# Linear attention into a gated MLP on one core: first weight block in two halves, far chunks projected in pairs, inputs stored in load order

## The chip, the cores and the metric

The kernel runs on one core of one Trainium2 chip. The metric is device time in microseconds (us) from launch to end; lower is better. The five engines are named as in the profile: PE (TensorE), ACT (ScalarE), DVE (VectorE), POOL (GpSimd) and SP (SyncE, which here only issues DMAs).

## What is computed

```
# q, k, v: (4, 4, 1088, 32); S1, S2: (8, 32); w_in: (128, 2048); w_out: (2048, 128)
def phi(x):                                  # 8 x 8 = 64 features
    a = einsum('rd,bhsd->bhsr', S1, x); b = einsum('rd,bhsd->bhsr', S2, x)
    return einsum('bhsi,bhsj->bhsij', a, b).reshape(..., 64)
q_p, k_p = phi(q), phi(k)
kv = einsum('bhsf,bhsd->bhfd', k_p, v);  z = sum(k_p, axis=2)
num = einsum('bhsf,bhfd->bhsd', q_p, kv)
den = einsum('bhsf,bhf->bhs', q_p, z)[..., None] + 1e-06
x = (num / den) with heads side by side      # (4352, 128)
h = x @ w_in;  g = h * clip(h + 3, 0, 6) / 6;  out = g @ w_out
```

## The kernel before

The 4352 tokens are cut into 9 chunks (`CHUNKS`, lines 38 and 39): eight of 512 tokens and a last one of 256. The keys and values of the four batches come in two groups per batch (`KGROUPS`, k0 to k7 and v0 to v7). All inputs lie in DRAM in pieces, one DMA each, and are loaded by SP (line 323).

The attention part has three kinds of step. `keys(b)` (from line 397) makes the key features of a batch (`mm_k`, `cp_k`, `outer_k`), sums them with the values over nine tiles (`kvt_b_i`, lines 405 and 408) and folds the sum into two small matrices (`twice`, `fold`, `keep`; for batch 0 also `spread`, `zmm`, `halves`, lines 427 to 436). `queries(c)` serves chunk 0 alone (`mm_q0`, `outer_q0`, `tr`, `nd`, `norm`, `xt`, lines 475 to 518). `far_queries(c)` serves chunks 1 to 8 (line 520): `proj_c` (line 533) projects one chunk on PE with small 32x32 matmuls into two banks of PSUM, DVE transposes them (`cp`, line 536), POOL and DVE form quotient and features (`prod`, `invert`, `divide`, `outer`, `turn`), eight small DMAs move them (`move_c`, line 574), and `xmm_c` (line 579) multiplies with the folded sum, again small matmuls of one chunk into two banks. `split` then writes x as a high and a low part (`xhi`, `xlo`).

The MLP part has 72 steps, one for each chunk c and pair fp of the eight pairs of 128 columns of w_in. In a step PE makes h from three products (`h_` and `l_`: lines 608, 609, 612), ACT and DVE make the gate (`relu`, line 619; `gate`, line 622), ACT rounds it (`ghi`, line 625), POOL or DVE takes the rest (`glo`, line 628), and PE adds six products with w_out to the chunk's sum (`o_` and `p_`, line 645). These matmuls use the whole array; below they are called the dense ones, and the small ones of attention the tiled ones.

The weights arrive as 64-bit floats in blocks of 512 columns (wi0 to wi3, wo0 to wo3) and are turned by hand into two 32-bit parts, seven instructions a block: `scale` and `rest` on ACT (lines 337, 340), `sign` and `shift` on DVE (343, 347), `word` on POOL (351), `high` on ACT (354), `low` on POOL (357). A step with pair fp waits for its block.

Three 16-element loads on ACT's queue (`peek`, line 258) touch three inputs at the start. Nothing is scheduled by the compiler: `ORDER` (lines 97 to 157) is a list of step names, and each engine and SP's queue take their instructions in that order. A suffix (`:V`, `:h`) picks an engine or a bank. `Plan.run` (line 189) gives each step its buffers from `BUFS`, first free first.

Of the kernel before, what the change touches and what calls it, by code (L numbers as in the profile page):

```python
# [97 lines left out]
warm ld_q0 warm warm mm_q0 ld_k0 cp_q0 ld_k1 mm_k0:h cp_k0 ld_v0 ld_wi1 ld_v1 outer_q0_0:V mm_k1 cp_k1 tr_0_0:o trcp_0_0 rest_wi1 scale_wi1 s_rep  # L98
s_copy outer_k1_0 outer_k0_2:V outer_k0_0:V outer_q0_2:V outer_k1_2:V outer_k1_4 kvt_0_0 kvt_0_1 kvt_0_2 s_tr kvt_0_3 kvt_0_4 kvt_0_5 kvt_0_6 kvt_0_7
kvt_0_8 s_back twice_0 fold_0 sign_wi1:h shift_wi1 spread zmm tr_0_2 word_wi1 ld_wi0 rest_wi0 scale_wi0 sign_wi0:o shift_wi0 word_wi0 halves nd_0_0:o  # L100
trcp_0_2 keep_0 high_wi1 ld_q1 ld_wo1 ld_k2 ld_k3 high_wi0 nd_0_2:h ld_wi2 low_wi1 norm_0_0 proj_1 xt_0_0:o ld_v2 low_wi0 ld_v3 ld_k4 ld_wi3 norm_0_2
xt_0_2 xhi_0_1 xhi_0_0 cp_1_0 mm_k2 ld_k5 cp_1_1 ld_wo0 sign_wo1:o scale_wo1 cp_k2 mm_k3 cp_k3 rest_wo1 prod_1 xlo_0_1 xlo_0_0 h_0_3_0 l_0_3_0 h_0_3_1
l_0_3_1 outer_k2_0 shift_wo1 h_0_0_1_0 l_0_0_1_0 h_0_0_1_1 l_0_0_1_1 h_0_0_0_0 invert_1 outer_k3_4:V outer_k2_2:V kvt_1_0:o kvt_1_1 l_0_0_0_0
h_0_0_0_1 sign_wi2 relu_0_3 word_wo1 scale_wi2 divide_1 outer_1_1 outer_1_0 gate_0_3 l_0_0_0_1 h_0_2_1 l_0_2_1 h_0_2_0 shift_wi2 outer_k3_0:V
outer_k3_2:V kvt_1_2 kvt_1_3 kvt_1_4 kvt_1_5 kvt_1_6 rest_wi2 relu_0_0 high_wo1 ghi_0_3 word_wi2 kvt_1_7 kvt_1_8 twice_1 high_wi2 mm_k4 l_0_2_0
low_wo1 fold_1 o_0_3 turn_1_0 turn_1_1 gate_0_0 h_0_1_1_0 low_wi2 l_0_1_1_0 h_0_1_1_1 h_0_1_0_0 l_0_1_1_1 l_0_1_0_0 move_1 h_0_1_0_1 l_0_1_0_1
relu_0_2 keep_1 scale_wi3 cp_k4 rest_wi3 sign_wi3:o ld_q3 gate_0_2 h_0_4_0 l_0_4_0 h_0_4_1 l_0_4_1 glo_0_3 mm_k5 ghi_0_2 p_0_3 o_0_2 outer_k4_0:V
shift_wi3 outer_k4_2:V word_wi3 relu_0_1 scale_wo0 cp_k5 relu_0_4 high_wi3 ld_v4 ld_q2 ld_v5 ghi_0_0 sign_wo0:o gate_0_1 h_0_5_1 h_0_5_0 l_0_5_1
l_0_5_0 relu_0_5 outer_k5_4:V outer_k5_0:V outer_k5_2:V xmm_1 xhi_1_0 glo_0_2 low_wi3 p_0_2 xhi_1_1 rest_wo0 gate_0_4 h_0_6_1 l_0_6_1 h_0_6_0 l_0_6_0
relu_0_6 ghi_0_4 shift_wo0 xlo_1_0 xlo_1_1 gate_0_5 proj_3 kvt_2_0 kvt_2_1 kvt_2_2 kvt_2_3 glo_0_0 word_wo0 high_wo0 low_wo0 h_1_2_0 h_1_2_1 l_1_2_1  # L110
l_1_2_0 relu_1_2 cp_3_0 ghi_0_1 gate_0_6 h_1_1_0 l_1_1_0 h_1_1_1 l_1_1_1 glo_0_4:V relu_1_1 cp_3_1 gate_1_2 kvt_2_4 kvt_2_5 kvt_2_6 kvt_2_7 proj_2
kvt_2_8 o_0_1 ld_q8 ld_v6 ld_k7 ld_wo2 ld_wo3 ld_q5 glo_0_1:V gate_1_1 ghi_1_2 h_1_3_1 h_1_3_0 l_1_3_0 l_1_3_1 ghi_1_1 relu_1_3 twice_2 scale_wo2
h_1_0_1 l_1_0_1 p_0_1 h_1_0_0 o_0_0 p_0_0 prod_3 invert_3 cp_2_0 fold_2 glo_1_2:V divide_3 rest_wo2 outer_3_1 glo_1_1 outer_3_0 cp_2_1 l_1_0_0 keep_2
prod_2 o_1_2 proj_5 gate_1_3 sign_wo2:h shift_wo2 word_wo2 ghi_1_3 relu_1_0 turn_3_1 cp_5_0 h_0_7_1 l_0_7_1 h_0_7_0 o_1_1 l_0_7_0 gate_1_0 h_1_5_0
invert_2 h_1_5_1 l_1_5_0 glo_1_3:V ghi_0_6 relu_0_7 p_1_2 l_1_5_1 cp_5_1 o_1_3 p_1_1 high_wo2 relu_1_5 out_0_3 divide_2 ghi_0_5 low_wo2 gate_0_7
h_1_4_0 turn_3_0 h_1_4_1 l_1_4_1 gate_1_5 p_0_4 l_1_4_0 h_1_7_0 h_1_7_1 l_1_7_0 ghi_1_0 glo_0_5:V scale_wo3 relu_1_4 rest_wo3 sign_wo3 shift_wo3
gate_1_4 ld_q4 ld_v7 ld_k6 move_3 ld_q6 o_0_4 p_0_5 ghi_0_7 proj_4 o_0_5 outer_2_1 glo_1_0 word_wo3 ghi_1_5 high_wo3 outer_2_0 low_wo3 cp_4_1 cp_4_0
# [619 lines left out]
```

## Time and profile before

| | |
|---|---|
| median of 3 runs | 230.46 us (230.12 to 230.94) |
| the profiled execution's own time | 230.75 us |
| its span, first to last instruction | 229.0 us |
| PE busy | 221.2 us, 97% of the span |
| DVE, ACT, POOL busy | 73%, 72%, 66% of the span |
| read from HBM | 11.30 MB |

The span is what the trace covers; 1.75 us of the profiled execution lie outside it. PE's busy time counts matmuls with their modelled ends, so two that overlap in the pipeline count once, and a high share does not say that each matmul runs at its best pace.

### The profile page before, as it was taken

The page shows a single profiled execution, that of the slowest core. Times are in us where ns is not written, and L with a number is a line of the kernel's source. Part 1 is how long each engine was busy: PE and PEld are TensorE (multiplying, and loading weights), DVE is VectorE, ACT ScalarE, POOL GpSimd, SP SyncE. Part 2 cuts the span into 40 slices and gives each one's busy share as a digit, 9 for nine tenths or more (in the row PEclk, how much of TensorE's full clock was granted, in tenths as well). Part 3 has the DMA queues.
Part 4 walks back from the last instruction along what each step waited for, and adds up shares of the span by engine and source line. Part 5 has one row for each costly group of instructions (what it writes and reads, how often), then busy time and mean ns, then how long its engine had stood idle before and what let it go on. Part 6 is the DMA issues. An engine that isn't in the chain of part 4 may idle for free.

```text
span 229.0 us, 4745 instructions
## 1 busy us (share of the span) xinstructions
PE 221.2 (97%) x1880; PEld 174.4 (76%) x1880; DVE 166.7 (73%) x215; ACT 166.0 (72%) x228; POOL 151.0 (66%) x108
## 2 busy tenths in 40 slices
PE   4899999999999999999999999999999999999994
PEld 2767867768687788777778788787888788888984
DVE  1789999999779768548869968885483577575552
ACT  3579998869778776877578666687585866778662
POOL 3289998496994599996077754037749615776480
PEclk9999999999999999999999999999999999999999
DMA  6995249701412001401200031212002000001001
GB/s 204 401 407 173 61 134 345 265 3 34 105 33 61 0 3 34 151 3 29 66 0 1 3 91 48 92 26 69 0 23 69 3 0 0 37 11 46 0 4 69
DMA packets 9382, 17.77 MB, mean 78 GB/s; under 512 B 1808, under 2 KB 2448, under 8 KB 9360
## 3 DMA queue, kind: packets, MB, share of 16 engines
q1 hardware_dynamic: 9264, 17.46, 23.0%
q8 instruction: 15, 0.25, 0.4%
q14 instruction: 7, 0.06, 0.1%
q10 hardware_dynamic: 96, 0.00, 0.0%
HBM read 11.30 MB, written 2.23 MB: 59 GB/s over the span
## 4 chain that ended last, share of the span: by engine, by line
PE 91%; DVE 2%; DMA 2%; ACT 2%; issue 1%; SPq 1%; ACTq 0%
PE o L645 42%; PE h L608 14%; PE h L612 13%; PE h L609 13%; PE a L579 2%; DMA kT<-kT_dram 2%; PE o L405 2%; PE a L533 2%; PE a L375 2%; ACT r L340 1%; DVE g L622 0%; PE o L489 0%; DVE kph L385 0%; DVE x L507 0%; SPq L323 0%
## 5 line engine op out<-in xcount | busy, mean ns | idle before, releaser
L628 POOL TENSOR_TENSOR gl<-g,gh 128x1024 fp32r<-128x1024 f32 (+1 forms) x41 | 95.7, 2349 | 49.6 <-ACT gh L625 31.9
L622 DVE SCALAR_TENSOR_TENSOR g<-g,h 128x1024 f32<-128x1024 f32 (+1 forms) x72 | 82.8, 1155 | 44.4 <-ACT g L619 44.1
L619 ACT ACTIVATE g<-h 128x1024 f32<-128x1024 f32 (+1 forms) x72 | 70.3, 981 | 34.1 <-PE h L612 21.7
L625 ACT CAST gh<-g 128x1024 fp32r<-128x1024 f32 (+1 forms) x72 | 70.9, 1003 | 13.0 <-PE o L645 6.6
L608 PE MATMUL h<-xh,wi_hi 128*128 128x512 f32 (+1 forms) x148 | 56.0, 380 | 0.5 <-DVE g L622 0.5
L645 PE MATMUL o<-gh,wo_hi 128*128 128x512 f32 (+1 forms) x144 | 54.9, 384 | 0.0
L609 PE MATMUL h<-xh,wi_lo 128*128 128x512 f32 (+1 forms) x148 | 54.9, 373 | 0.0
L645 PE MATMUL o<-gh,wo_lo 128*128 128x512 f32 (+1 forms) x144 | 54.1, 378 | 0.0
L612 PE MATMUL h<-xh,wi_hi 128*128 128x512 f32 (+1 forms) x148 | 51.1, 375 | 0.0
L645 PE MATMUL o<-gl,wo_hi 128*128 128x512 f32 (+1 forms) x144 | 41.3, 380 | 0.0
L628 DVE TENSOR_TENSOR gl<-g,gh 128x1024 fp32r<-128x1024 f32 (+1 forms) x31 | 38.2, 1244 | 2.4 <-ACT gh L625 2.3
L608 PEld LDWEIGHTS h<-xh,wi_hi 128*128 128x128 f32 x148 | 27.8, 188 | 8.2 <-DVE g L622 1.1
L645 PEld LDWEIGHTS o<-gh,wo_hi 128*128 128x128 f32 x144 | 27.1, 188 | 6.5 <-issue 0.8
L612 PEld LDWEIGHTS h<-xh,wi_hi 128*128 128x128 f32 x148 | 27.5, 188 | 5.3
L609 PEld LDWEIGHTS h<-xh,wi_lo 128*128 128x128 f32 x148 | 27.8, 188 | 4.8
L645 PEld LDWEIGHTS o<-gh,wo_lo 128*128 128x128 f32 x144 | 27.1, 188 | 4.8
L645 PEld LDWEIGHTS o<-gl,wo_hi 128*128 128x128 f32 x144 | 25.8, 188 | 5.4 <-issue 0.8
L562 POOL TENSOR_TENSOR qph<-ab 128x512 f32<-128x512 f32 (+1 forms) x16 | 19.9, 1257 | 0.3
L351 POOL TENSOR_TENSOR w<-w,r 128x512 int32<-128x512 int32 x8 | 10.3, 1290 | 1.9 <-DVE w L347 1.9
L569 DVE STREAM_TRANSPOSE raw<-qph 128x512 f32<-128x512 f32 (+1 forms) x16 | 10.5, 665 | 0.3 <-POOL qph L562 0.3
L543 POOL TENSOR_TENSOR prods<-ab 128x128 f32<-128x128 f32 (+1 forms) x8 | 4.5, 557 | 7.0 <-DVE den L547 5.0
L385 POOL TENSOR_TENSOR kph<-ab 128x512 f32<-128x512 f32 (+1 forms) x6 | 5.5, 928 | 4.2 <-ACT ab L378 4.2
(95 smaller groups left out, 162.5 us busy)
## 6 DMA issues: line engine op xcount, KB each, us to landing
phT<-raw SPq DMA_DIRECT2D x56, 64.0 KB, 2.0
qT<-qT_dram SPq DMA_DIRECT2D x8, 256.0 KB, 3.1
raw<-w_in_dram SPq DMA_DIRECT2D x4, 512.0 KB, 7.7
raw<-w_out_dram SPq DMA_DIRECT2D x4, 512.0 KB, 7.0
outT_dram<-os SPq DMA_DIRECT2D x8, 256.0 KB, 2.2
v<-v_dram SPq DMA_DIRECT2D x4, 330.0 KB, 5.1
kT<-kT_dram SPq DMA_DIRECT2D x4, 320.0 KB, 5.1
v<-v_dram SPq DMA_DIRECT2D x4, 264.0 KB, 5.0
```

Source lines behind the costliest of these rows:

```text
L351: nc.gpsimd.tensor_tensor(w, w, at(rb), op=ALU.add)
L385: engines[e].tensor_tensor(out, a_, b_, op=ALU.mult)
L562: engines[e].tensor_tensor(out, a_, b_, op=ALU.mult)
L569: nc.vector.transpose(turned_view()[:, :, r * half : (r + 1) * half].rearrange("p f (t w) -> p t f w", w=Q), src)
L608: nc.tensor.matmul(at(hb)[:, u, i:k], wi_hi[:, f], x, start=True, stop=False)
L609: nc.tensor.matmul(at(hb)[:, u, i:k], wi_lo[:, f], x, start=False, stop=False)
L612: nc.tensor.matmul(at(hb)[:, u, i:k], wi_hi[:, f], at(x_buf[c])[:, 1, i:k], start=False, stop=True)
L619: nc.scalar.activation(at(gb)[:, :, :n], at(hb)[:, :, :n], AF.Relu, bias=3.0, scale=1.0)
L622: nc.vector.scalar_tensor_tensor(at(gb)[:, :, :n], at(gb)[:, :, :n], 6.0, at(hb)[:, :, :n], op0=ALU.min, op1=ALU.mult)
L625: nc.scalar.copy(at(gh)[:, :, :n], at(gb)[:, :, :n])
L628: engines[e].tensor_tensor(at(gl)[:, :, :n], at(gb)[:, :, :n], at(gh)[:, :, :n].bitcast(F32), op=ALU.subtract)
L645: nc.tensor.matmul(at(ob)[:, :n], w, x[:, :n], start=left == acc["all"] and i == 0, stop=left == 1 and i == len(pairs) - 1)
```

## The change

The table `BLOCKS` lets a weight block have any width: w_in's first 512 columns are now two blocks of 256 (wi0, wi1), and the old wi1, wi2, wi3 are called wi2, wi3, wi4. `FAR` groups the far chunks: chunk 1 alone, (2, 3), (4, 5), (6, 7), chunk 8 alone; a group has one `proj` step and one `xmm` step on PE, each still with two banks, where a chunk takes 256 columns of each bank. What lies between is per chunk, as before. There is a fourth `ab` buffer, a bank of a pair may be of the `o` kind, and one of the three warm-up matmuls (`warm`) and the three `peek` loads are gone. The inputs lie in two DRAM arrays, tokens and weights, in the order of their loads. `ORDER` is a new list throughout.

```
-BUFS = dict(... ab=3, ...)
+BUFS = dict(... ab=4, ...)
-NWB = DFF // WB
+BLOCKS = dict(wi=(0, 256, 512, 1024, 1536, DFF), wo=tuple(range(0, DFF + 1, WB)))
+FAR = ((1,), (2, 3), (4, 5), (6, 7), (8,))
...
-warm ld_q0 warm warm mm_q0 ld_k0 cp_q0 ld_k1 mm_k0:h cp_k0 ld_v0 ld_wi1 ...
+ld_k0 warm s_rep s_tr mm_k0:h ld_wi0 scale_wi0 warm s_back ld_k1 mm_k1 ...
...
-    peek(peeked[:, 0:1], kT, 9 * P)
-    peek(peeked[:, 1:2], v1, 9 * H * DV)
-    peek(peeked_w, w_in[P * WB :], WB)
...
+    def place(name):
+        source, i, j = places[name]
+        return inputs[source][i:j].rearrange("(p x) -> p x", p=P)
...
-            nc.sync.dma_start(view(at(b)), src)
+            nc.sync.dma_start(view(at(b)), place(name))
...
-    def far_queries(c):
+    def far_queries(cs):
...
-        pbs, xpbs = [Buf(("a",)), Buf(("a",))], [Buf(("a",)), Buf(("a",))]
+        pbs, xpbs = ([Buf(("a", "o")) for _ in range(2)] for _ in range(2))
...
+        def part(banked, k, r, i, j):
+            return bank(banked[r])[:, k * half + i - r * half : k * half + j - r * half]
+
+        def proj(_):
+            for (k, r, b, i, j), h in product(spans, range(H)):
+                e, g = h * Q, (h ^ r) * Q
+                nc.tensor.matmul(part(pbs, k, r, i, j)[g : g + Q], s_proj[e : e + Q, b, :], at(projected[k])[e : e + Q, i:j], ...)
+        projected_by = plan.add(f"proj_{label}", PE, [*loads, *done], proj, [*projected, *pbs])
+        for k, c in enumerate(cs):
+            moves.append(quotient(c, n, projected_by, [(pbs[r], k * half) for r in range(2)], moved[k]))
+        xhs = [Buf(("xh",)) for _ in cs]
+        o = plan.add(f"xmm_{label}", PE, [*moves, *done], xmm, [*moved, *xpbs, *xhs])
...
+    places, arrays = {}, {"tokens": [], "weights": []}
+    for name in ["sb", *(word[3:] for word in ORDER.split() if word.startswith("ld_"))]:
```

Two places show how instructions move. The first is PE around the projection of chunks 2 and 3 (qT is a chunk's queries, a and o the banks, kph and ab the key features of batch 2). Before, from `proj_3` on:

```order
L533 MATMUL a_72<-qT_83,s_proj 32x256 x4
L533 MATMUL a_73<-qT_83,s_proj 32x256 x4
L405 MATMUL o_70<-kph_88,v_127 32x64 x4
L408 MATMUL o_70<-ab_84 32x32
L405 MATMUL o_70<-kph_88,v_127 32x64 x4
L408 MATMUL o_70<-ab_84 32x32
```

and, twelve dense matmuls later, around `proj_2`:

```order
L405 MATMUL o_70<-kph_87,v_128 32x64 x4
L408 MATMUL o_70<-ab_85 32x32
L533 MATMUL a_72<-qT_81,s_proj 32x256 x4
L533 MATMUL a_73<-qT_81,s_proj 32x256 x4
L405 MATMUL o_70<-kph_87,v_128 32x64 x4
L408 MATMUL o_70<-ab_85 32x32
L645 MATMUL o_71<-gh_104,wo_hi 128x512
```

Now, with the last product of step (0, 3) ahead of it (gl is what `glo_0_3` leaves):

```order
L664 MATMUL o_70<-gh_105,wo_lo 128x512
L664 MATMUL o_70<-gl_109,wo_hi 128x512 x2
L542 MATMUL o_71<-qT_81,s_proj 32x256 x4
L542 MATMUL a_73<-qT_81,s_proj 32x256 x4
L542 MATMUL o_71<-qT_83,s_proj 32x256 x4
L542 MATMUL a_73<-qT_83,s_proj 32x256 x4
L627 MATMUL h_68<-xh_95,wi_hi 128x512
```

The two projections stood at two places, one beside and one inside the sums of batch 2; now they follow each other, between dense matmuls, and the nine sums of batch 2 stand together later.

The second place is DVE at the start, from the key features of the second group of batch 0 to the quotient of chunk 0 (z_diag is written by `spread`, den and x by `norm`; raw is a loaded weight block). Before:

```order
L385 TENSOR_TENSOR kph_88<-h_68,ab_85 128x512 x2
L385 TENSOR_TENSOR qph_89<-a_72,ab_84 128x512
L385 TENSOR_TENSOR kph_87<-a_73,ab_86 128x512
L343 TENSOR_SCALAR h_69<-raw_74 128x512
L347 SCALAR_TENSOR_TENSOR w_118<-w_118,h_69 128x512
L427 TENSOR_TENSOR z_diag<-mask,o_71 128x256
L343 TENSOR_SCALAR o_70<-raw_75 128x512
L347 SCALAR_TENSOR_TENSOR w_119<-w_119,o_70 128x512
L504 TENSOR_SCALAR den_122<-o_71 128x8
```

Now:

```order
L385 TENSOR_TENSOR kph_89<-a_73,ab_85 128x512 x2
L385 TENSOR_TENSOR qph_90<-h_69,ab_86 128x512 x2
L343 TENSOR_SCALAR o_70<-raw_76 128x512
L427 TENSOR_TENSOR z_diag<-mask,o_71 128x256
L347 SCALAR_TENSOR_TENSOR w_120<-w_120,o_70 128x512
L343 TENSOR_SCALAR o_70<-raw_77 128x512
L347 SCALAR_TENSOR_TENSOR w_119<-w_119,o_70 128x512
L504 TENSOR_SCALAR den_123<-a_72 128x8
```

Behind the second group's copy (ab_86 before, ab_85 now) DVE had one instruction of key features, then a weight block's two with z_diag behind them; now it has four of features and one of a weight block ahead of z_diag. Between z_diag and den three weight instructions stand in place of two.

## Rows read from the trace of the kernel before

**Rows 1.** The page, part 1: busy time of each engine and its share.
```profile
PE 221.2 (97%) x1880; PEld 174.4 (76%) x1880; DVE 166.7 (73%) x215; ACT 166.0 (72%) x228; POOL 151.0 (66%) x108
```
**Rows 2.** PE's waits from 17 us to the end: total, times, longest.
```profile
PE h L608 <- DVE g L622: 0.5, 1, 0.5
```
**Rows 3.** The chain that ended last, first 16 us: start us, us, what.
```profile
2.12 4.60 DMA kT<-kT_dram
...
6.75 1.33 PE a L375 x20
...
11.58 0.43 DVE z_diag L427
...
15.13 0.44 DVE x L507
```
**Rows 4.** Instructions in order of time: start us, us, engine, line, operation, tiles.
```profile
5.43 1.07 PE L375 MATMUL h<-s_all,kT 128*64 128x64 f32 x16
...
6.55 0.37 ACT L378 COPY ab<-h 128x256 f32<-128x256 f32 x1 [0.48 <-PE h L375]
...
6.95 1.29 DVE L385 TENSOR_TENSOR kph<-h,ab 128x512 f32<-128x512 f32 x2 [0.16 <-ACT ab L378]
...
8.13 0.43 ACT L378 COPY ab<-a 128x320 f32<-128x320 f32 x1 [1.21 <-PE a L375]
...
8.64 1.66 POOL L385 TENSOR_TENSOR kph<-ab 128x512 f32<-128x512 f32 x2 [3.64 <-ACT ab L378]
...
11.74 1.28 POOL L351 TENSOR_TENSOR w<-w,r 128x512 int32<-128x512 int32 x1 [1.44 <-DVE w L347]
...
11.91 0.69 DVE L343 TENSOR_SCALAR o<-raw 128x512 uint32<-128x512 uint32 x1
...
15.97 1.25 PE L375 MATMUL a<-s_all,kT 128*32 128x64 f32 x72
...
17.15 0.50 PE L608 MATMUL h<-xh,wi_hi 128*128 128x512 f32 x1
```
**Rows 5.** The same view of PE, at its wait after the first dense matmuls.
```profile
21.39 0.50 PE L608 MATMUL h<-xh,wi_hi 128*128 128x512 f32 x1 [0.53 <-DVE g L622]
```
**Rows 6.** The same view of PE, around one projection of a chunk.
```profile
103.97 0.39 PE L645 MATMUL o<-gh,wo_lo 128*128 128x512 f32 x1
104.29 0.66 PE L533 MATMUL a<-qT,s_proj 32*32 32x256 f32 x16
104.88 0.50 PE L608 MATMUL h<-xh,wi_hi 128*128 128x512 f32 x1
105.22 0.40 PE L609 MATMUL h<-xh,wi_lo 128*128 128x512 f32 x1
105.45 0.40 PE L612 MATMUL h<-xh,wi_hi 128*128 128x512 f32 x1
```
**Rows 7.** Groups by line and shape: count, busy us, mean ns of one, idle before.
```profile
L628 POOL TENSOR_TENSOR gl<-g,gh 128x1024 fp32r<-128x1024 f32 x38 | 92.0, 2433 | 44.5 <-ACT gh L625 31.9 <-PE o L645 9.7 <-ACT g L619 2.9
...
L536 DVE STREAM_TRANSPOSE ab<-a 128x256 f32<-128x256 f32 x14 | 5.8, 427 | 1.1 <-ACT g L619 0.6 <-PE a L533 0.3
...
L533 PE MATMUL a<-qT,s_proj 32*32 32x256 f32 x112 | 4.6, 386 | 0.0
...
L533 PE MATMUL a<-qT,s_proj 32*32 32x64 f32 x32 | 0.5, 220 | 0.0
```
**Rows 8.** SP's queue in order of time: start us, us of the issue, what.
```profile
4.02 0.43 SPq L323 DMA_DIRECT2D raw<-w_in_dram  x1
...
5.09 0.72 SPq L323 DMA_DIRECT2D raw<-w_out_dram  x1
5.86 1.26 SPq L323 DMA_DIRECT2D kT<-kT_dram  x2
```
**Rows 9.** DMA issues near 4.0, 5.1 and 6.7 us: size, us from issue to landing.
```profile
raw<-w_in_dram SPq DMA_DIRECT2D x1, 512.0 KB, 6.7
...
raw<-w_out_dram SPq DMA_DIRECT2D x1, 512.0 KB, 7.5
...
kT<-kT_dram SPq DMA_DIRECT2D x1, 320.0 KB, 8.9
```

More of the change, by code (lines that the diff above doesn't have):

```diff
@@ L97 @@
 ORDER = """
[L98 to L117, printed above, removed]
@@ L154 @@
-glo_7_7:V glo_8_7:V p_8_7 p_7_7 ghi_7_5 relu_8_5 relu_8_1 o_7_2 gate_8_5 h_8_6_1 h_8_6_0 l_8_6_0 ghi_8_5 gate_8_1 l_8_6_1 h_8_4_0 relu_8_6 o_7_5
-glo_8_3 l_8_4_0 p_8_3 h_8_4_1 l_8_4_1 glo_7_5 ghi_8_1 p_7_5 o_8_1 gate_8_6 relu_8_4 p_7_4 ghi_8_6 gate_8_4 glo_8_1 glo_8_6:V o_8_7 p_8_1 o_8_6
-glo_8_5:V o_8_5 ghi_8_4 glo_8_4:V p_8_6 p_8_5 o_8_4 store_5 store_6 out_7_7 store_7 p_8_4 out_8_7 store_8
+ld_k0 warm s_rep s_tr mm_k0:h ld_wi0 scale_wi0 warm s_back ld_k1 mm_k1 sign_wi0:o shift_wi0 rest_wi0 cp_k0 outer_k0_2 ld_wi1 sign_wi1 outer_k0_0:V
@@ new lines @@
+word_wi0 ld_q0 rest_wi1 scale_wi1 shift_wi1 high_wi0 cp_k1 word_wi1 ld_v0 mm_q0:h ld_v1 ld_wi2 outer_k1_2:V outer_k1_0:V outer_k1_4 kvt_0_0 kvt_0_1
+kvt_0_2 kvt_0_3 kvt_0_4 kvt_0_5 kvt_0_6 kvt_0_7 kvt_0_8 high_wi1 cp_q0 outer_q0_0:V outer_q0_2:V tr_0_0 sign_wi2:o ld_wo1 rest_wi2 twice_0 spread
+s_copy low_wi1 scale_wi2 low_wi0 fold_0 zmm trcp_0_0 scale_wo1 halves tr_0_2:o shift_wi2 nd_0_0 sign_wo1:o shift_wo1 word_wi2 trcp_0_2 rest_wo1
+high_wi2 keep_0 ld_q1 ld_k3 ld_k2 ld_wi3 ld_v2 ld_k5 ld_v3 nd_0_2:h norm_0_0 ld_wi4 norm_0_2 xt_0_0:h proj_1:a:o xt_0_2 low_wi2:V cp_1_0 cp_1_1
@@ L203, in run @@
             assert all(n.name in done for n in op.needs) and name not in done, name
-            engine = {"A": ACT, "V": DVE, "G": POOL}.get(choice, op.engines[0])
+            engine = op.engines[0]
+            if choices and choices[0] in "AVG":
+                engine = {"A": ACT, "V": DVE, "G": POOL}[choices.pop(0)]
             for b in op.bufs:
                 if b.slot < 0:
-                    b.tag = choice if choice in b.tags else b.tags[0]
+                    b.tag = choices.pop(0) if choices and len(b.tags) > 1 else b.tags[0]
                     b.slot = free[b.tag].popleft()
@@ L518, in queries, with xmm @@
         split(c, [(0, 0, n // 2, last[:1], xps), (n // 2, n // 2, n, last[1:], xps)], xh)
-    def far_queries(c):
-        c0, n = CHUNKS[c]
+    def far_queries(cs):
+        n = CHUNKS[cs[0]][1]
         half, blocks = n // 2, n // 2 // Q
-        cuts = [i for i in range(n) if i in (0, half) or batch_of(c0 + i) != batch_of(c0 + i - 1)] + [n]
-        spans = [(i // half, batch_of(c0 + i), i, j) for i, j in zip(cuts, cuts[1:])]
-        lq, qb = load("qT", f"q{c}", stretch(qT, c0, c0 + n), lambda t: t[:, :n])
-        pbs, xpbs = [Buf(("a",)), Buf(("a",))], [Buf(("a",)), Buf(("a",))]
-        ab, ph, turned, phT, xh, den, rden = (Buf((g,)) for g in ("ab", "qph", "raw", "phT", "xh", "den", "den"))
+        pbs, xpbs = ([Buf(("a", "o")) for _ in range(2)] for _ in range(2))
+        label = "".join(str(c) for c in cs)
+        spans, loads, projected, moved, moves = [], [], [], [], []
+        for k, c in enumerate(cs):
+            c0 = CHUNKS[c][0]
+            cuts = [i for i in range(n) if i in (0, half) or batch_of(c0 + i) != batch_of(c0 + i - 1)] + [n]
+            spans += [(k, i // half, batch_of(c0 + i), i, j) for i, j in zip(cuts, cuts[1:])]
+            lq, qb = load("qT", f"q{c}", lambda t: t[:, :n])
+            loads.append(lq)
+            projected.append(qb)
+            moved.append(Buf(("phT",)))
+        done = [kv_done[b] for b in sorted({b for _, _, b, _, _ in spans})]
+        def part(banked, k, r, i, j):
[3 more added lines that the diff above has]
+                e, g = h * Q, (h ^ r) * Q
+                nc.tensor.matmul(part(pbs, k, r, i, j)[g : g + Q], s_proj[e : e + Q, b, :], at(projected[k])[e : e + Q, i:j], start=True, stop=True, tile_position=(e, g))
+        def xmm(_):
+            for (k, r, b, i, j), h in product(spans, range(H)):
+                e, g = (h ^ r) % 2 * HP, h * Q
+                nc.tensor.matmul(part(xpbs, k, r, i, j)[g : g + Q], kvs[b][e : e + HP, g : g + Q], at(moved[k])[e : e + HP, h // 2, i:j], start=True, stop=True, tile_position=(e, g))
+        projected_by = plan.add(f"proj_{label}", PE, [*loads, *done], proj, [*projected, *pbs])
+        for k, c in enumerate(cs):
+            moves.append(quotient(c, n, projected_by, [(pbs[r], k * half) for r in range(2)], moved[k]))
+        xhs = [Buf(("xh",)) for _ in cs]
+        o = plan.add(f"xmm_{label}", PE, [*moves, *done], xmm, [*moved, *xpbs, *xhs])
+        for k, c in enumerate(cs):
+            split(c, [(k * half, r * half, (r + 1) * half, [o], xpbs[r]) for r in range(2)], xhs[k])
@@ L528, in far_queries, with quotient @@
+    def quotient(c, n, o, sources, phT):
+        half, blocks = n // 2, n // 2 // Q
+        ab, ph, turned, den, rden = (Buf((g,)) for g in ("ab", "qph", "raw", "den", "den"))
         prodb = Buf(("prod",))
-        def proj(_):
-            for (r, b, i, j), h in product(spans, range(H)):
-                e, g = h * Q, (h ^ r) * Q
-                nc.tensor.matmul(bank(pbs[r])[g : g + Q, i - r * half : j - r * half], s_proj[e : e + Q, b, :], at(qb)[e : e + Q, i:j], start=True, stop=True, tile_position=(e, g))
@@ L535, in cp @@
         def cp(_, r):
-            nc.vector.transpose(at(ab)[:, r * half : (r + 1) * half], bank(pbs[r])[:, :half])
+            src, i = sources[r]
+            nc.vector.transpose(at(ab)[:, r * half : (r + 1) * half], bank(src)[:, i : i + half])
         def parts():
@@ L574, in move @@
                 nc.sync.dma_start(at(phT)[e : e + Q, g // 2, :n], turned_view()[g * Q : (g + 1) * Q, f, :n])
-        def xmm(_):
-            for (r, b, i, j), h in product(spans, range(H)):
-                e, g = (h ^ r) % 2 * HP, h * Q
-                nc.tensor.matmul(bank(xpbs[r])[g : g + Q, i - r * half : j - r * half], kvs[b][e : e + HP, g : g + Q], at(phT)[e : e + HP, h // 2, i:j], start=True, stop=True, tile_position=(e, g))
-        done = [kv_done[b] for b in sorted({b for _, b, _, _ in spans})]
-        o = plan.add(f"proj_{c}", PE, [lq, *done], proj, [qb, *pbs])
-        cps = [plan.add(f"cp_{c}_{r}", DVE, [o], partial(cp, r=r), [pbs[r], ab]) for r in range(2)]
+        cps = [plan.add(f"cp_{c}_{r}", DVE, [o], partial(cp, r=r), [sources[r][0], ab]) for r in range(2)]
         o = plan.add(f"prod_{c}", POOL, cps, prod, [ab, prodb])
@@ L588, in far_queries @@
         turns = [plan.add(f"turn_{c}_{r}", DVE, outers[r : r + 1], partial(turn, r=r), [ph, turned]) for r in range(2)]
-        o = plan.add(f"move_{c}", SP, turns, move, [turned, phT])
-        o = plan.add(f"xmm_{c}", PE, [o, *done], xmm, [phT, *xpbs, xh])
-        split(c, [(0, r * half, (r + 1) * half, [o], xpbs[r]) for r in range(2)], xh)
+        return plan.add(f"move_{c}", SP, turns, move, [turned, phT])
     sums = {}
@@ L676, in step @@
             sums[c, "part"] = a, osb
-    for j in range(NWB):
-        weights("wi", w_in, wi_hi, wi_lo, j)
-        weights("wo", w_out, wo_hi, wo_lo, j)
+    for nm, *w in (("wi", wi_hi, wi_lo), ("wo", wo_hi, wo_lo)):
+        for j in range(len(BLOCKS[nm]) - 1):
+            weights(nm, *w, j)
     for b in range(B):
         keys(b)
-    for c in range(len(CHUNKS)):
-        queries(c) if c < NEAR else far_queries(c)
+    for c in range(NEAR):
+        queries(c)
+    for cs in FAR:
+        far_queries(cs)
     for c, fp in product(range(len(CHUNKS)), range(NPAIR)):
@@ L695, in words @@
         return np.ascontiguousarray(a).view(np.int64)
-    def stretches(a, cuts):
-        return np.concatenate([a[:, i:j].reshape(-1) for i, j in zip([0, *cuts], [*cuts, a.shape[1]])])
-    groups = [t0 * P for t0, _ in KGROUPS[1:]]
-    starts = [c for c, _ in CHUNKS[1:]]
-    blocks = range(WB, DFF, WB)
     qT = q.transpose(1, 3, 0, 2)
```

174 lines of the change are left out of this document (99 added, 75 removed).

## The prediction

> **What bounds the kernel.** I read the page's busy times first: PE is busy 97% of the span, the others 66 to 76% [rows 1]. Then PE's waits: from 17 us to the end PE waits once, 0.5 us, for a gate of DVE [rows 2]; it stands behind the first dense matmuls [rows 5]. So the time is three things: when the first dense matmul starts (17.15 us [rows 4]), what PE issues after it, and those 0.5 us. The other engines' work costs only where it makes PE wait. Third, PE in order of time around a small block, to see what lies between matmuls though PE counts as busy [rows 6]. Last, the chain of the start [rows 3], its instructions [rows 4] and the loads [rows 8, 9].
>
> The matmuls that compute are the same before and after, one to one; dense ones follow each other every 0.23 us (105.22 to 105.45 [rows 6]). Their total cannot change. What can are the edges between dense and tiled work, the start, and new waits.
>
> **Pairs, and tiled work put together: minus 2.1 us.** An edge is seen around a projection [rows 6]. Into it: the dense matmul at 103.97 should be followed at 104.20, the projection starts at 104.29, so 0.09. Out of it: a tiled record of 256 columns lasts 386 ns and one of 64 columns 220 [rows 7], so 192 columns take 166 ns and 256 take 0.22 us; the rest of a record is its drain. The 16 records last 0.66 together, so the last starts at 104.56 and has streamed at 104.78; the dense one starts at 104.88 (0.10) and its follower 0.34 after it, where 0.23 is normal (0.11). Out costs 0.21. The whole block costs 105.22 - 0.23 - 104.20 = 0.79, of which two rounds of 0.22 stream.
>
> In the two orders of instructions, after the first dense matmul, I count the edges: from dense to tiled 22 before and 17 now, back also five fewer, and between kinds of tiled work (sums next to a projection) 8 before and 4 now. Six come from merging projections 2 with 3, 4 with 5, 6 with 7 and the same xmm; the others from the sums of batch 2 and a key step that stand together. The edges between tiled kinds I price at the middle of in and out, 0.15. Sum: 5 x 0.09 + 5 x 0.21 + 4 x 0.15 = 2.1. The low end counts only the five ways out, 1.0; the high end takes all 14 edges at 0.21, 2.9. I take 2.1, because a second route agrees: a pair should cost 0.79 + 0.44 = 1.23 instead of 1.58, 0.35 less, and six pairs give 2.1. What these steps hand to DVE, POOL and SP is the same in number: transposes, quotients and eight moves per chunk.
>
> **Start: plus 1.1 us.** The change reorders it all. k1, the load on which the chain hangs, lands at 2.12 + 4.60 = 6.72 [rows 3]; ahead of it stood q0 and k0, now k0 and wi0, both 912 KB with k1 and the 80 KB of sb, so I keep 6.72. Its projection ends at 8.08 [rows 3] in both. Then:
> - Before, ACT copied it at 8.13 for 0.43 [rows 4]. Now ACT has `high_wi0` ahead of that copy. `mm_k0` (1.07) comes first or second on PE, ending about 6.3; copy 0.37, then on POOL `outer_k0_2` (some 1.1 of the 1.66 for 512 and 256 columns) to 7.8, `word_wi0` (half of 1.28) to 8.4 [rows 4], the cast about 0.4. The copy ends near 9.2, not 8.56: 0.65 later.
> - DVE then has four feature products (1.29 for two [rows 4]) to 11.8, `sign_wi2` (0.69 less 0.07 of overlap) to 12.4, and z_diag, ending at 12.85. Before it ended at 12.01 [rows 3]: 0.8 later.
> - Between z_diag and the quotient of chunk 0 stand three weight instructions of DVE, not two: 12.85 + 3 x 0.69 = 14.9. The quotient's second x then comes at 15.13 + 1.0 [rows 3].
> - `low_wi2` now runs on DVE (about 0.69 as its neighbours) ahead of the transposes that free a bank for `mm_k3`; of the 1.25 us of `mm_k2` and `mm_k3` [rows 4] the first half runs under it. First dense matmul near 18.25 instead of 17.15: plus 1.1.
>
> Its bounds: 0, if the pieces overlap better, and 2.2, if every link is as late again. The removed warm-up matmul and the three peeks sit beside these waits; I cost them at nothing, because PE waits for sb at that time anyway. If that cover fails, it shows in k1's landing.
>
> **Two loads for one: 0.** SP issues one DMA more, 0.43 us of its queue [rows 8]; the data of the two halves are the same bytes as one block and the load behind them is the same number of bytes away. The queue is never empty then, so the issue is hidden by transfers in flight. The Trainium skill's page "DMA: Bandwidth & Descriptors", section Rules for kernel authors, speaks against it: for bandwidth it wants large transfers, and it counts a fixed cost of some 2 us for each DMA. By that the sum would be 2 us worse if it lay on the path; here the loads follow each other with their issues overlapping [rows 8], so I leave it out. The order in DRAM: no row shows its worth; I take 0, with half a microsecond to each side.
>
> **Waits of PE: 0.** The 0.53 us [rows 5] go, because dense work starts later while DVE's gate does not move as far. New: the low product of step (0, 3) now stands right behind the high one, and its operand comes from POOL, 2.43 us [rows 7], behind a weight block's last instruction. I estimate 0.5 for it and the gate together, from 0 to one POOL instruction less the dense work ahead, 1.3. Late next is then POOL, not DVE. After 50 us I find no step whose supply moves nearer to PE than before. The end (last product, `out`, store) is the same.
>
> **Sum:** -2.1 + 1.1 - 0.5 + 0.5 = -1.0. The profiled execution took 230.75, so 229.75; it stood 0.29 over the median, so **229.5 us** against 230.46. About 0.3% (0.7 us) can be told from no change: faster is below 229.77, slower above 231.15. Forecast, chance 0.55, its own range 228.9 to 230.1.
>
> **Rivals.**
> - *Pairs save only their ways out* (0.18): the second chunk pays its own fill inside the block. For it: I have no row of two projections in a row. Against: records overlap within one. -1.0 + 1.1 = 230.5.
> - *wo1 holds up the start; slower* (0.11). `scale_wo1` now stands on ACT ahead of `halves`, which everything of chunk 0 needs near 13.4. By bytes wo1 lands between 10.7 (2530 KB, 4.02 + 6.7) and 12.6 (3298 KB, 5.09 + 7.5) [rows 8, 9], at 3042 KB about 12.0, in time. But k3, issued by 6.75, took 8.9 [rows 8, 9] and landed at 15.6, two microseconds behind that pace. From 13.4 on each microsecond costs one. If wo1 lands at 14.6, first dense work is 2.3 late: -2.1 + 2.3 + 0.5 = +0.7, 231.2.
> - *The start is not later* (0.12): with fewer arrays and no peeks k1 lands a microsecond earlier, or ACT finds room. Then -2.1 stays: 228.4. Against: the loads run back to back from 4 us on in the order of rows 8.
> - *A wait for banks* (0.04). A pair fills two banks for two chunks, and DVE must empty them with four transposes of 0.43 [rows 7], 1.7 us, before PE's next user of the bank. After projections 2 and 3 that is `xmm_1`, behind 16 dense matmuls, 3.7 us. It decides only where DVE is 2 us behind. At half a microsecond for each of three pairs: 231.0. The Trainium skill's page "TensorEngine Tiling (Array Packing)", section PSUM Bottleneck, is behind this one: tiling speeds the matmuls, not the emptying of PSUM. By that rule the pairs would give their gain back; the 3.7 against 1.7 speak against it here.
>
> **How the numbers follow.** Of the forecast 0.47 lie below 229.77 and 0.08 above; with 0.12 of the early start that makes faster 0.59. Same is 0.08 + 0.18 = 0.26, slower 0.11 + 0.04 = 0.15. For 8 in 10 the range goes down to 228.2, a little below the early start, and up to 230.9, which takes in the first rival and leaves most of the slower ones out.
>
> **What would show it.** Right: projection blocks of 32 records of about 1.1 us and dense work 0.34 behind them; first dense matmul between 18.0 and 18.5; z_diag near 12.4; PE waiting 0.3 to 0.8 us behind 23 us, for POOL or DVE, and nowhere later. Wrong: a pair of twice 0.66; wo1's conversion waiting for its load; waits of PE after 50 us; or a first dense matmul after 19.5, which would cost what the pairs bring.

## The result, and the profile of the changed kernel

The changed kernel takes **228.92 us** (median of 10 runs, 228.17 to 230.14), the kernel before 230.77 in the same set: a ratio of 0.991, 95% interval 0.9886 to 0.9935. It is faster, by more than the 0.3% that can be told from no change. The profiled execution took 228.8 us with a span of 227.0.

The page, part 1, of the changed kernel, beside [rows 1]:

```profile
PE 219.1 (97%) x1879; PEld 176.5 (78%) x1879; DVE 163.4 (72%) x216; ACT 166.0 (73%) x231; POOL 153.7 (68%) x111
```

PE's busy share is as it was. Its list of waits from 17 us to the end, where [rows 2] held one, is empty. So what changed is the start and what PE spends between matmuls that compute, though it counts as busy there.

The start, in order of time (start us, us, engine, line, operation, tiles); it is to be read beside [rows 3, 4]:

```profile
6.43 1.34 PE L375 MATMUL a<-s_all,kT 128*64 128x64 f32 x20 [0.28 <-DMA kT<-tokens_dram]
...
7.90 0.40 ACT L354 CAST wi_hi<-w 128x256 fp32r<-128x256 f32 x1
8.21 0.42 ACT L378 COPY ab<-a 128x320 f32<-128x320 f32 x1
...
11.98 0.42 DVE L427 TENSOR_TENSOR z_diag<-mask,o 128x256 f32<-128x256 f32 x1
...
14.08 0.69 DVE L347 SCALAR_TENSOR_TENSOR w<-w,o 128x512 uint32<-128x512 uint32 x1
14.78 0.17 DVE L504 TENSOR_SCALAR den<-a 128x8 f32<-128x8 f32 x1
...
17.02 1.23 PE L375 MATMUL a<-s_all,kT 128*32 128x64 f32 x72
18.18 0.50 PE L627 MATMUL h<-xh,wi_hi 128*128 128x512 f32 x1
```

The first dense matmul comes at 18.18 where it came at 17.15 [rows 4]: 1.03 later. The end of PE, from the chain that ended last, first of the changed kernel, then of the kernel before:

```profile
219.46 4.33 PE o L664 x36
```
```profile
221.62 4.28 PE o L645 x32
```

PE ends at 223.79 and not at 225.90. From the first dense matmul to that end it needs 205.6 us where it needed 208.7. In these 3.1 us lies the gain; the start takes 1.03 of it back.

Two places show most of it. First a pair (projections 4 and 5) in PE's order of time, to be read beside the single one of [rows 6]:

```profile
50.66 0.61 PE L664 MATMUL o<-gl,wo_hi 128*128 128x512 f32 x2
51.20 0.42 PE L542 MATMUL a<-qT,s_proj 32*32 32x256 f32 x4
51.23 0.42 PE L542 MATMUL o<-qT,s_proj 32*32 32x256 f32 x4
...
51.90 0.39 PE L542 MATMUL o<-qT,s_proj 32*32 32x256 f32 x4
52.22 0.50 PE L627 MATMUL h<-xh,wi_hi 128*128 128x512 f32 x1
52.56 0.39 PE L628 MATMUL h<-xh,wi_lo 128*128 128x512 f32 x1
```

The second dense matmul of the first row starts at 50.88 and streams until 51.11; the block costs 52.56 - 0.23 - 51.11 = 1.22. Two single ones cost 2 x 0.79 [rows 6]. Second, the place where a new wait was foreseen, POOL and then PE:

```profile
25.58 2.42 POOL L647 TENSOR_TENSOR gl<-g,gh 128x1024 fp32r<-128x1024 f32 x1
```
```profile
27.70 0.40 PE L664 MATMUL o<-gh,wo_lo 128*128 128x512 f32 x1
28.05 0.73 PE L664 MATMUL o<-gl,wo_hi 128*128 128x512 f32 x2
```

POOL ends at 28.00 and PE goes on at 28.05. Without a wait it would have gone on at 27.93 (27.70 + 0.23), so the wait is 0.12.

### The profile page after: what moved, and what is told of

Read it like the earlier page. It is cut to its first block, busy times and chain, and to the rows that moved or that the text cites. A ratio compares the mean times of both kernels' runs of the same rounds, so it can differ in the third digit from the quotient of the medians.

```text
span 227.0 us, 4743 instructions
## 1 busy us (share of the span) xinstructions
PE 219.1 (97%) x1879; PEld 176.5 (78%) x1879; DVE 163.4 (72%) x216; ACT 166.0 (73%) x231; POOL 153.7 (68%) x111
## 4 chain that ended last, share of the span: by engine, by line
PE 92%; DMA 3%; ACT 2%; SPq 1%; issue 1%; ACTq 0%
PE o L664 41%; PE h L627 15%; PE h L631 14%; PE h L628 14%; DMA raw<-weights_dram 3%; PE a L547 2%; PE o L405 2%; PE a L375 2%; SPq L322 1%; PE a L542 1%; ACT r L340 1%; PE o L542 0%; ACT w L337 0%; PE h L511 0%; ACT phT L493 0%
## 5 line engine op out<-in xcount | busy, mean ns | idle before, releaser
L647 POOL TENSOR_TENSOR gl<-g,gh 128x1024 fp32r<-128x1024 f32 (+1 forms) x45 | 106.2, 2372 | 56.8 <-ACT gh L644 38.5
L638 ACT ACTIVATE g<-h 128x1024 f32<-128x1024 f32 (+1 forms) x72 | 70.6, 980 | 35.3 <-PE h L631 20.8
L644 ACT CAST gh<-g 128x1024 fp32r<-128x1024 f32 (+1 forms) x72 | 70.2, 1001 | 11.2 <-DVE g L641 6.3
L664 PE MATMUL o<-gh,wo_hi 128*128 128x512 f32 (+1 forms) x144 | 54.2, 379 | 0.0
L647 DVE TENSOR_TENSOR gl<-g,gh 128x1024 fp32r<-128x1024 f32 (+1 forms) x27 | 33.0, 1233 | 5.9 <-PE o L664 3.6
L590 POOL TENSOR_TENSOR qph<-ab 128x512 f32<-128x512 f32 (+1 forms) x16 | 16.1, 1016 | 0.2
L351 POOL TENSOR_TENSOR w<-w,r 128x512 int32<-128x512 int32 (+1 forms) x9 | 10.4, 1164 | 3.3 <-DVE w L347 2.6
L597 DVE STREAM_TRANSPOSE raw<-qph 128x512 f32<-128x512 f32 (+1 forms) x16 | 10.4, 663 | 1.9 <-POOL qph L590 1.9
L385 DVE TENSOR_TENSOR kph<-a,ab 128x512 f32<-128x512 f32 (+1 forms) x14 | 8.8, 634 | 0.2 <-ACT ab L378 0.2
L340 ACT ACTIVATE r<-raw 128x512 int32<-128x512 uint32 (+1 forms) x9 | 5.6, 627 | 1.9 <-DMA raw<-weights_dram 1.9
```

Source lines behind the costliest of these rows:

```text
L351: nc.gpsimd.tensor_tensor(w, w, at(rb)[:, :n], op=ALU.add)
L385: engines[e].tensor_tensor(out, a_, b_, op=ALU.mult)
L590: engines[e].tensor_tensor(out, a_, b_, op=ALU.mult)
L597: nc.vector.transpose(turned_view()[:, :, r * half : (r + 1) * half].rearrange("p f (t w) -> p t f w", w=Q), src)
L638: nc.scalar.activation(at(gb)[:, :, :n], at(hb)[:, :, :n], AF.Relu, bias=3.0, scale=1.0)
L644: nc.scalar.copy(at(gh)[:, :, :n], at(gb)[:, :, :n])
```

## The experiments

Ten more kernels ran, the last of them once. Below, F is the start of the first dense matmul in the profiled execution and R the time from there to PE's last end. The column k1 is the start of the projection of k1. It waits for that load, except in four kernels where the load is there before PE is done with the work ahead: projections paired, both unsplit ones, and DRAM by name.

| kernel | time, us | ratio to before, 95% | k1 | F | R |
|---|---|---|---|---|---|
| before | 230.8 | 1 | 6.75 | 17.15 | 208.7 |
| changed | 228.92 | 0.991 (0.9886 to 0.9935) | 6.43 | 18.18 | 205.6 |
| pairs broken | 232.47 | 1.0058 (1.0036 to 1.0081) | 6.21 | 17.74 | 209.2 |
| pairs broken, earlier piece | 231.07 | 1.0021 (1.0002 to 1.0041) | 6.27 | 17.58 | 207.7 |
| broken in 14 places | 238.63 | 1.033 (1.0296 to 1.0363) | 7.51 | 18.74 | 215.3 |
| before, projections paired | 231.16 | 1.0026 (1.0001 to 1.0051) | 6.29 | 16.66 | 209.5 |
| unsplit block | 231.36 | 1.0015 (0.9983 to 1.0046) | 6.13 | 20.33 | 206.0 |
| unsplit, copy first | 229.20 | 0.9939 (0.9918 to 0.996) | 6.16 | 18.62 | 206.0 |
| wo1 behind | 235.05 | 1.0174 (1.0148 to 1.0199) | 7.07 | 18.64 | 211.3 |
| peeks back | 228.66 | 0.990 (0.9872 to 0.9927) | 7.24 | 18.45 | 205.5 |
| DRAM by name | 229.00 | 0.9928 (0.9906 to 0.9951) | 6.87 | 18.27 | 205.6 |
| sums broken | 229.46, one run | | 6.13 | 17.53 | 206.8 |

### Is it the pairs? They are broken again

One piece of dense work stands between the two chunks of each pair; banks, loads and shapes stay.

```
- xmm_23 ... p_0_5 h_1_4_1
+ xmm_23_0 p_0_5 xmm_23_1 ... h_1_4_1
```

> The changed kernel (228.9 us), with one piece of dense work (2 to 4 matmuls) put between the two chunks of each of the six pairs; banks, loads and everything else stay. If the gain comes from edges between dense and tiled work, each break costs an edge in and an edge out, 0.30 to 0.35 us: six make plus 1.8 to 2.1, so 230.7 to 231.0 us, 0.999 to 1.001 of the kernel before; each block of 16 records then costs 0.79 in place of half of 1.22. Rival: the pairs bring nothing and the gain lies in the waits and the order around them: 228.6 to 229.3, and two blocks cost together what the pair costs.

Measured: 232.47, plus 3.55. The theory has the direction and is short by 1.4; the rival is out. Each broken pair costs 0.79 + 0.80 in place of 1.22. The rest came in with the edit: small waits, and some of it that no single row shows. The largest piece is at the first pair:

```profile
29.25 0.50 PE L632 MATMUL h<-xh,wi_hi 128*128 128x512 f32 x1 [0.36 <-DVE w L347]
```

A dense step that is pulled 0.4 us forward needs a bank that DVE still uses. To see whether the remainder is of this kind, the same six breaks were made the other way round, with the first chunk moved *ahead* of the dense step that stood in front of the pair (five of the six):

```
- o_0_4 ... xmm_23 ... p_0_5
+ xmm_23_0 o_0_4 ... xmm_23_1 ... p_0_5
```

> The six pairs broken once more, but for five of them the first chunk's matmuls are moved ahead of the dense step that stood in front of the pair, so that no dense step comes earlier than in the changed kernel and none can meet an operand that isn't ready. If the first run's plus 3.5 us was six breaks of 0.37 and otherwise waits that its own edit brought (dense steps pulled 0.4 us forward), this one costs 6 x 0.37 = 2.2 plus at most 0.4: 231.1 to 231.5 us, 1.001 to 1.003 of the kernel before. Rival: a break costs 0.59 wherever it is put: 232.4 again.

Measured: 231.07, 2.15 over the changed kernel and at the low edge of what was expected; PE has no wait in its list. Projections 4 and 5 in that run:

```profile
50.29 0.42 PE L542 MATMUL a<-qT,s_proj 32*32 32x256 f32 x4
...
50.56 0.39 PE L542 MATMUL o<-qT,s_proj 32*32 32x256 f32 x4
50.88 0.73 PE L669 MATMUL o<-gl,wo_hi 128*128 128x512 f32 x2
51.54 0.42 PE L542 MATMUL a<-qT,s_proj 32*32 32x256 f32 x4
...
52.13 0.50 PE L632 MATMUL h<-xh,wi_hi 128*128 128x512 f32 x1
52.47 0.39 PE L633 MATMUL h<-xh,wi_lo 128*128 128x512 f32 x1
```

R is 2.1 us longer than in the changed kernel, 0.35 for each pair. With the pairs broken the time is that of the kernel before to 0.2%: the pairs carry the whole gain, and all else in the change adds up to about nothing (a later start against shorter waits and less other tiled work).

### What does a break cost that lies inside a chunk?

> As the run before, with 14 breaks in place of 6 (chunks of four of the pairs broken in their middle too, 8 records to a piece). If a break costs an edge whatever the size of the piece: 14 x 0.30 to 0.35 = plus 4.2 to 4.9 over the changed kernel, 233.1 to 233.8 us (1.010 to 1.013 of the kernel before). Rival: it is each chunk's own fill that costs, not the break: about as much as six breaks, 230.7 to 231.0. Rival: the breaks hide behind other work: 229.

```
- proj_23 h_0_5_1 h_0_5_0 l_0_5_1
+ proj_23_0_0 h_0_5_1 proj_23_0_1 h_0_5_0 proj_23_1_0 l_0_5_1 proj_23_1_1
```

Measured: 238.63, plus 9.7; all three expectations missed. As the edit stands, nine of the 14 breaks lie inside chunks and five between them. Half of one chunk, and then two halves together, one of each chunk of the pair, from that run:

```profile
53.57 0.63 PE L543 MATMUL a<-qT,s_proj 32*32 32x256 f32 x8
54.14 0.73 PE L670 MATMUL o<-gl,wo_hi 128*128 128x512 f32 x2
54.80 0.42 PE L543 MATMUL o<-qT,s_proj 32*32 32x256 f32 x4
...
55.07 0.39 PE L543 MATMUL a<-qT,s_proj 32*32 32x256 f32 x4
```

8 records take 0.63 us (53.57 to 54.20), 16 take 0.66 (54.80 to 55.46). The two halves run side by side, on different tiles of the array; a half alone takes as long as both. The edit leaves 16 pieces of 8 records, 0.77 each as a block, and four of 16, 0.79 each, where there were six pairs: 16 x 0.77 + 4 x 0.79 - 6 x 1.22 = 8.2. Of the other 1.5, the list of PE's waits names 0.7; the rest is open.

### Pairs alone, in the order of the kernel before

```
- proj_3 kvt_2_0 ... cp_3_1 ... proj_2 ... cp_2_0 ... cp_2_1
+ proj_23 kvt_2_0 ... cp_3_1 cp_2_0 cp_2_1
```

> The kernel before (230.8 us), with its own start, loads and order; only projections 2 and 3, 4 and 5, 6 and 7 are made pairs in shared banks (ab gets its fourth buffer, four banks' transposes move behind the pair, one load moves behind a projection); the products xmm stay single. If pairs save edges: 0.37 for each of two, 0.54 for 2 and 3, which stood between the sums of batch 2: minus 1.3, so 229.5 us, 0.994 of the kernel before. Rival: the gain of the changed kernel is not in the pairs: 230.5 to 231.1. Rival: the later transposes and quotients make PE wait: above 231.

Measured: 231.16, and the second rival holds. The pairs of 4 and 5 and of 6 and 7 cost 1.22 here too. The pair of 2 and 3, whose singles had stood beside and inside the sums of batch 2, saves only 0.1 of the 0.54 expected, with 0.2 of waiting for a load in it. And PE waits 1.4 us for DVE's gates, three times, where the kernel before had one wait of 0.5, which is still among them. One of the two new ones, DVE and then PE:

```profile
37.55 2.22 DVE L643 TENSOR_TENSOR gl<-g,gh 128x1024 fp32r<-128x1024 f32 x1
39.70 1.10 DVE L553 STREAM_TRANSPOSE ab<-a 128x256 f32<-128x256 f32 x3
40.72 1.18 DVE L637 SCALAR_TENSOR_TENSOR g<-g,h 128x1024 f32<-128x1024 f32 x1
```
```profile
41.95 0.50 PE L623 MATMUL h<-xh,wi_hi 128*128 128x512 f32 x1 [0.28 <-DVE g L637]
```

Three transposes in a row, which empty the pair's two banks, stand ahead of a gate that PE needs. They are not alone: the low product ahead of them took 2.22 us, and in the kernel before the one at this place took 1.22:

```profile
37.63 1.22 DVE L628 TENSOR_TENSOR gl<-g,gh 128x1024 fp32r<-128x1024 f32 x1
```

PE could have gone on at 41.50 (the matmul ahead starts at 41.27) and did at 41.95. By these rows I estimate that the gate would have been in time either with a product of 1.22 or with one transpose in place of three; no run parts the two. The Trainium skill, "TensorEngine Tiling (Array Packing)", section PSUM Bottleneck, says that after a speed-up by tiling the copies out of PSUM may become the bottleneck. The trace of this run agrees in part, with 1.1 us of transposes ahead of the gate. But four in a row need not cost anything: these of projections 6 and 7 in the changed kernel make PE wait for nothing.

```profile
101.46 1.44 DVE L564 STREAM_TRANSPOSE ab<-a 128x256 f32<-128x256 f32 x4 [1.58 <-PE a L542]
```

### The split block

```
- wi=(0, 256, 512, 1024, 1536, DFF)
+ wi=(0, 512, 1024, 1536, DFF)
```

In `ORDER` one block's steps, at about the place of the second half's, take the place of two blocks' steps.

> The changed kernel with the first block of w_in loaded and converted as one of 512 columns, at the place of its second part; k1 then has 256 KB less ahead of it. If the split is worth nothing, as the prediction has it: 228.5 to 229.4 us. Rival: the split carries the start, because the first part is converted while DVE and ACT wait for k1 anyway; then about half a block of DVE work (0.43 + 0.41 us) and of ACT work falls behind k1 and the first dense matmul comes 0.5 to 0.9 later: 229.4 to 229.8. Rival from the large-transfer rule: one load is better, k1 lands 0.5 earlier and the start gains that, 228.4.

Measured: 231.36, plus 2.4, more than any theory had. ACT, DVE, and the granted clock by stretches (us of the stretch, PE busy, clock, share and rate of DMA):

```profile
10.95 0.62 ACT L353 CAST wi_hi<-w 128x512 fp32r<-128x512 f32 x1 [1.78 <-POOL w L350]
11.48 0.36 ACT L377 COPY ab<-h 128x256 f32<-128x256 f32 x1
```
```profile
11.87 1.29 DVE L384 TENSOR_TENSOR qph<-h,ab 128x512 f32<-128x512 f32 x2 [1.10 <-ACT ab L377]
```
```profile
12.00:14.00 2.00, 0.94 (x13) 1.00 1.06 419
14.00:14.50 0.50, 0.36 (x4) 1.00 0.98 378
14.50:18.00 3.50, 3.41 (x40) 0.51 1.04 414
```

The cast now waits for a whole block on POOL, and the copy of q0 waits behind the cast in ACT's queue, though its operand is ready; DVE waits 1.10 us for it. PE has less to do meanwhile, and from 14.5 to 18 us the granted clock is 0.51, the level of 1.2 GHz. To part the block's width from the place of the copy, one more kernel has the copy ahead of the cast:

```
- high_wi0 cp_q0
+ cp_q0 high_wi0
```

> The run with the unsplit block (231.4 us; DVE waited 1.10 us for the copy of q0, which stood behind the cast of the 512 columns on ACT), with that copy put ahead of the cast and nothing else changed. If the split was worth that place in ACT's queue: the feature products of q0 start 1.1 earlier, the first dense matmul comes near 19.2 in place of 20.33, and, if TensorE then is not granted the lower clock in the start, near 18.4: 229.2 to 230.3 us. Rival: loading and converting 512 columns late is itself what costs (DVE, POOL and the load): 231 as before.

Measured: 229.20, at the low edge of what was expected. The two steps in ACT's order, and PE's stretch from 14 to 18 us, where the clock is now whole:

```profile
9.38 0.37 ACT L377 COPY ab<-h 128x256 f32<-128x256 f32 x1 [0.30 <-PE h L374]
10.88 0.62 ACT L353 CAST wi_hi<-w 128x512 fp32r<-128x512 f32 x1 [1.13 <-POOL w L350]
```
```profile
14.00:18.00 4.00, 3.26 (x89) 1.00 1.03 409
```

With the copy there, the split is worth 0.3 us, which is not clear of the noise: the intervals overlap. A queue position was worth 2.2, the lower clock behind it included. Against the split spoke the rule of the Trainium skill, "DMA: Bandwidth & Descriptors", section Rules for kernel authors (large transfers). Here one load of 512 columns gains nothing over two of 256 (229.20 against 228.92). The fixed cost of some 2 us that the prediction quotes from this page of the Trainium skill is fitted there (section Anatomy of one DMA, SWDGE path) to loads that GpSimd issues, and these loads are issued by SP.

### What held up the start

```
- scale_wo1 halves ... sign_wo1:o shift_wo1 ... rest_wo1 ... norm_0_0 ... word_wo1 high_wo1 low_wo1
+ halves ... norm_0_0 ... xlo_0_1 sign_wo1:o shift_wo1 ... word_wo1 ... relu_0_0 high_wo1 low_wo1
```

> The changed kernel, with the conversion of the block wo1 (scale, sign, shift, rest, word, high, low) taken out of the start and put behind the split of x of chunk 0. By the prediction's reading (DVE's weight instructions between z_diag and the quotient hold up the start) the first dense matmul comes 0.7 to 1.4 earlier, near 17.2; the stall behind the first dense matmuls may come back with 0.3 to 0.7: 228.0 to 228.7 us. Rival: the chain of ACT and PE (copies of kvb and phT, products nd) bounds the start, and DVE is only just late: 0.3 earlier, 17.9, and 228.5 to 229.3.

Measured: 235.05; both missed. F is 11.57 behind k1 and was 11.75: the start gains 0.2, less than this difference varies between kernels with the same start (11.2 to 11.75). DVE, and then two of PE's waits of that run (total, times, longest):

```profile
15.25 0.17 DVE L503 TENSOR_SCALAR den<-a 128x8 f32<-128x8 f32 x1 [1.66 <-PE a L498]
```
```profile
PE o L404 <- POOL kph L384: 2.4, 1, 2.4
PE o L663 <- POOL gl L646: 0.5, 1, 0.5
```

Without wo1 DVE stands idle 1.66 us for the products `nd`, so its weight instructions did not hold the quotient up. The products wait for the copies of ACT, and these for PE. The price is paid later: POOL takes wo1 ahead of the feature products of k3, PE waits 2.4 us, and the mean granted clock of the stretch in which it waits is 0.86 (us of the stretch, PE busy, clock, share and rate of DMA):

```profile
24.00:28.00 4.00, 1.70 (x52) 0.86 0.00 0
```

The early place of wo1 is what keeps POOL free at 20 us.

### The peeks and the order in DRAM

> The changed kernel with three small loads of 16 partitions issued on ACT's queue ahead of all else, as the kernel before has them. If their removal is worth nothing (the prediction): 228.6 to 229.3 us. Rival: ACT loads its table only behind these three issues (2.13 us before, 0.73 after), so s_all comes 0.8 later, and with it the projection of k0, the feature products on POOL, and the copy of k1 behind the cast on ACT: the first dense matmul up to 0.8 later, 229.4 to 229.8.

```
+ peek(peeked[:, 0:1], "k2"); peek(peeked[:, 1:2], "v2"); peek(peeked_w, "wi2")
```

> The changed kernel with the pieces of its two input tensors laid out by name (sb, queries, keys and values, w_in, w_out) in place of the order in which they are loaded. If the order in DRAM is worth nothing: k1 lands at 6.2 to 6.7 us and the time is 228.5 to 229.4 us. Rival: neighbouring pieces are read faster: k1 lands 0.3 or more later and the start with it, 229.3 to 229.8.

```
- for name in ["sb", *(word[3:] for word in ORDER.split() if word.startswith("ld_"))]:
-     source, piece = pieces[name]
+ for name, (source, piece) in pieces.items():
```

Measured: 228.66 and 229.00, both nothing, as predicted. With the peeks back `s_all` starts at 4.12 and not 3.32; F less k1 is 11.21, no more than the other kernels of this order have.

### The sums

> The changed kernel with the sums of batch 2 and of batch 3 (kvt, 90 records each, 1.54 us in one block) broken once each by the last low product of a dense step (2 matmuls). If an edge between dense and tiled work costs the same for sums as for projections: each two blocks together 1.54 + 0.35 to 0.37 = 1.9 us. Rival: sums have their own way of filling, and the break is cheaper (under 0.2) or dearer (over 0.5).

The two steps l_0_7_1 and l_3_5_1 went into the middle of the sums. The block of batch 2, unbroken 1.54:

```profile
42.42 0.39 PE L631 MATMUL h<-xh,wi_hi 128*128 128x512 f32 x1
...
43.46 0.51 PE L631 MATMUL h<-xh,wi_hi 128*128 128x512 f32 x1
...
44.72 0.50 PE L627 MATMUL h<-xh,wi_hi 128*128 128x512 f32 x1
45.06 0.40 PE L628 MATMUL h<-xh,wi_lo 128*128 128x512 f32 x1
```

From 42.65 (the first dense matmul has streamed) to 44.83 (45.06 less 0.23), less 0.23 for the dense matmul inside, is 1.95: the break costs 0.41, a little more than expected and than between projections. R is 1.2 longer: two breaks, a new wait of 0.3 for a gate of DVE, and 0.1 more.

## Why the prediction was right, point by point

It said 229.5, faster with a chance of 0.59; measured 228.92, inside its range and at the low edge of the likeliest case. On the profiled execution it had minus 1.0; the trace has minus 2.0. By its terms:

- **Pairs and tiled work, minus 2.1.** Right in mechanism. The six pairs broken into single blocks cost 2.1 (R of the cleaner break, 207.7 against 205.6). Against the kernel before, all blocks of tiled work behind the first dense matmul, each counted as above, add up to 18.4 us and were 20.8: minus 2.3. The count of edges was right and one price a little low: with 0.35 for a way in and out in place of 0.30 it gives 5 x 0.35 + 4 x 0.15 = 2.35. That the second route gave the same 2.1 was chance. It has nothing for the sums and key steps, and it takes every single block of before as one that stood alone, where three of the twelve stood beside or inside sums.
- **The start, plus 1.1.** It measured 1.03, but by other links than named, and partly by luck: the prediction kept k1 where it was, and its projection started 0.32 earlier; from k1 on this profile has 1.35. The cast of the first half ended at 8.30, only just in the copy's way: the copy ended at 8.63, not 9.2. z_diag ended at 12.40, not 12.85. And the "three weight instructions of DVE" ahead of the quotient lay beside the chain of ACT and PE: without two of them nothing clear of the scatter is gained. That the chain and DVE ended together (DVE's shift at 14.77, the quotient at 14.78) made the wrong link give the right time. What the runs support: measured from k1, F comes 10.4 later in the two kernels with the old order, and 11.2 to 11.75 in the seven that have the new one untouched up to there, so the new start is 0.8 to 1.35 longer.
- **The old stall, minus 0.5.** It went. It had cost more than the 0.53 listed as idle: the matmul ahead of it starts at 20.59 and has streamed at 20.71, so 21.39 - 20.71 = 0.68.
- **The new wait, plus 0.5.** This term was furthest off: 0.12. The link was right, POOL's low product ends 0.05 before PE goes on; the half microsecond was a guess between 0 and 1.3.
- **Split block, peeks, DRAM order: 0.** Right within what can be told. But the split was worth 2.4 as long as the order around it stayed, which counting bytes could not show.
- **The rivals.** Pairs that save only their ways out: a pair costs 1.22, not more. wo1 late: it landed before ACT asked for it at 13.00. Start not later: it is. Waits for banks: none in the changed kernel; in the old order with pairs the transposes that empty the banks help to hold up DVE's gates.
- **Its signs.** The block of 32 records (1.09 us, and 0.34 between the two dense matmuls behind it), the time of the first dense matmul and the lack of later waits came as it said. z_diag started at 11.98, not near 12.4, and the wait was 0.12, not 0.3 to 0.8.

So 0.2 (tiled work), 0.2 (the old stall) and 0.4 (the new wait) were given away in the sum, all on the side of a smaller gain. The remaining 0.2 is spread over some 860 places where one dense matmul follows another, at a pace a little quicker than before; why is open.

## What to carry to other kernels

Where one engine is busy 97% and never waits, count its changes between kinds of work: here each way from dense to tiled work and back costs about 0.35 us (0.41 for sums), and putting two small blocks together saves that, provided the engine that empties their banks still has time for its other work. In a hand-made order a step's worth is that of its place in a queue: try the order with and without it, and move the step that waits before removing what it waits for. A cost read off two chains that end together cannot say which of them binds; take one away.
